# Attention and a mixture of experts on one core: the transposes of the attention take a float32r identity, and VectorE rounds a pair's k

## The chip, the cores and the metric

The kernel runs on one core of one Trainium2 chip. A core has five engines that run side by side, each with an instruction queue of its own: TensorE (PE; its weight loads are listed apart as PEld), VectorE (DVE), ScalarE (ACT), GpSimd (POOL) and SyncE (SP, which here only issues DMAs). The metric is the device time of one launch in microseconds (us).

## The reference

Eight batches of eight heads (sequence 576, head size 64) go through a causal attention with a decay: the score of query i and key j gets the sum of log f from j+1 to i added. The rows of the result then go through a mixture of eight experts, where each row takes one expert.

```
scores = matmul(q, k.T) / sqrt(D)
cum = cumsum(log(clip(f, 1e-4, 1)))
scores = where(causal, -1e9, scores + cum[..., :, None] - cum[..., None, :])
attn = exp(scores - max);  attn = attn / (sum(attn) + 1e-9)
x = matmul(attn, v)                      # 4608 rows of 512
expert = argmax(x @ w_gate);  gate = softmax(x @ w_gate)[expert]
out = gate * (relu(x @ w1[expert]) @ w2[expert])
```

All data are float32. A float32r value is a float32 word that TensorE is to take in its faster form for such words; before it is used so, an engine writes ("rounds") it in that type.

## The kernel before

**Pairs and steps.** The attention works on 32 pairs of heads, n = 0 to 31, four to a batch (p = n % 4). A pair has seven steps. In steps 0 to 4 TensorE makes the score tiles of both heads j by tile t of 128 queries: (0,3), (1,3), then (0,2) with (0,0), (1,2) with (1,0), and (0,1) with (1,1). Steps 5 and 6 make the two halves of a joint tile, which holds the last 64 queries of both heads. Each tile is the sum of two products (qk with qk, 128 rows, and k with q, 68 rows, L334), since q and k are each split in a rounded float32r part and the rest.

**What happens to a score.** VectorE's `s_red` (L341) reads the tile from PSUM, adds the mask, keeps the row's extreme and writes the tile to the buffer `sc` in SBUF. ScalarE's `s_exp` (L348) takes the exponential in place. One pair later TensorE transposes the tile in blocks of 128 x 128 (L402, L421, L432, L443: six groups of four and one single block per pair), and VectorE or ScalarE copies the transposed blocks from PSUM to `aT` (L391, L393). Another pair later `av` multiplies them with v (L472), and ScalarE copies the result to `xT` (L481). When a batch is done, its `xT` is transposed (L510, five groups of four per batch), scaled by VectorE (L520) and written out; its gate logits, `gT`, are transposed too (L560, five blocks per batch), and small operations of VectorE route the rows (L817 to L915).

**Operands.** For a later pair GpSimd rounds q (L289), takes the rest of q (L250), and copies the rounded q (L298). ScalarE rounds k (`k_first`, L293), and only then can GpSimd take the rest of k (L250, in `copies`). GpSimd's queue has these four in that order for each pair, and five more operations per batch for the routing (L897).

**Order.** The order of all work on each engine is the order in which the code issues it (`order.pin`). In a step, the code issues the scores of pair n, then the transposes of pair n-1, then the exponentials; k_first of pair n+1 comes at the end of step 1, ahead of `av`.

**Memory.** The score tiles of PSUM rotate through three banks (`ps_s`), the transposes through two (`ps_t`). `s_joint` puts the single transposed block of the pair before (L443) into the bank of its first half. So the second score tile of the next pair (step 1, 128x512) takes the bank that the first joint half (step 5, 128x288) leaves, once VectorE has read it.

**Experts.** From about 333 us on, TensorE runs the experts' matmuls (L1106, L1129) and transposes the gathered rows in groups of four; there the identity is float32r already (`identr`, L1071).

Of the kernel before, what the change touches and what calls it, by code (L numbers as in the profile page):

```python
# [57 lines left out]
def open_pools(c, ctx, tc):  # L58


    pool = lambda name, bufs, **k: ctx.enter_context(tc.tile_pool(name=name, bufs=bufs, **k))
    c.const = pool("const", 1)
    c.rp = pool("route_c", 1)
    c.rps = pool("route_s", 1)
    c.sm = pool("att_sm", 2)
    c.qp = pool("qk", 3)
    c.wp = pool("raw", 2)
    c.sp = pool("att_s", 2)
    c.xp = pool("xT", 2)
# [20 lines left out]
def setup_consts(c, tc):  # L90
    c.ident = c.const.tile([P, P], F32, name="ident")
    make_identity(tc.nc, c.ident)


def attention_all(c, tc, qkT, va, vb, f, wgd, x_dram, batch_done, more_consts, extra):
# [19 lines left out]
    with ExitStack() as st:  # L115
# [65 lines left out]

        cw = c.xp.tile([NH, 2, 640], F32R, name="cw", tag="xT")
        cwf = cw.bitcast(F32)
# [37 lines left out]
        wg = c.const.tile([P, NPAIR, 32], F32, name="wg")  # L221
        gT = c.const.tile([P, 5 * P], F32, name="gT")

        def late_consts():
            nc.gpsimd.memset(wg, 0.0)
            nc.gpsimd.memset(gT[:, S:], 0.0)
            more_consts()
# [7 lines left out]

        vts, xTs, ssums, jsums = {}, {}, {}, {}
        vbs = [io.tile([KB, 2, HD], F32, name=f"vb_{i}", bufs=1) for i in range(3)]
# [54 lines left out]
        def k_first(n):  # L292
            nc.scalar.copy(ops[n][0][:, QW:], raws[n][:, QW:])  # L293

# [26 lines left out]

        scs, nms, aTs = {}, {}, {}

        def s_begin(n):
            scs[n] = sp.tile([P, 2 * HW + S], F32, name="sc", tag="sc")
            nms[n] = sm.tile([P, 12], F32, name="nmx", bufs=3)
# [25 lines left out]
        def s_tiles(n, items):

            b, p = divmod(n, NPAIR)
            pb = psum(ps_s)
            o = 0
            for j, t in items:
                w = P * (t + 1)
                smm(pb[:, o : o + w], n, [(j, j * 640 + P * t)], 0, w)
                o += w  # L360
            o = 0
            for j, t in items:
                w = P * (t + 1)
                d = j * HW + SO[t]
                s_red(n, d, pb[:, o : o + w], mask[:, 512 - w :], 5 * j + t, 1.0e38)
                o += w

        def e_tiles(n, items):
            b, p = divmod(n, NPAIR)
            for j, t in items:  # L370
                s_exp(n, j * HW + SO[t], P * (t + 1), 5 * j + t,
                      ssums[b][:, t, 2 * p + j : 2 * p + j + 1])

        def s_joint(n, half):
            pb = psum(ps_s)
            smm(pb[:, 0:JW], n, [(0, 512), (1, 1152)], half * JW, JW)
            if half == 0 and n > 0:

                t_last(n - 1, pb[:, JW : JW + P])
            m = mask[:, 0:JW] if half == 0 else maskj  # L380
            s_red(n, half * JW, pb[:, 0:JW], m, 10 + half,
                  1.0e38 if half == 0 else nms[n][:, 10:11])
# [30 lines left out]

        def t_one(n, eng):
            aT, sc = aTs[n], scs[n]
            pt = psum(ps_t)
            for j in range(2):
                for k in range(2):
                    s0 = j * HW + SO[1] + P * k
                    o = P * (2 * j + k)  # L420
                    note(nc.tensor.transpose(pt[:, o : o + P], sc[:, s0 : s0 + P], c.ident))  # L421
            copy_on(
                eng, aT[:, :, P : P + 2 * AS].rearrange("p j (a q) -> p j a q", q=AS)[..., 0:P],
                pt.rearrange("p (j a q) -> p j a q", j=2, a=2),
            )

        def t_joint(n, eng):
            aT, sc = aTs[n], scs[n]
            pt = psum(ps_t)
            for k in range(4):  # L430
                s0 = P * k
                note(nc.tensor.transpose(pt[:, P * k : P * k + P], sc[:, s0 : s0 + P], c.ident))  # L432
# [26 lines left out]
        def av(n):  # L459
# [3 lines left out]
            for (qa, qb, nb), bank in zip(AV, (ps_v, ps_m)):  # L463
# [40 lines left out]
        def fin_x(b, t, scalar=False):  # L504
            xT, rinv = xTs[b], rinvs[b]
# [32 lines left out]
        def fin_gate(b):  # L538

            xT = xTs[b]  # L540
            for q0, q1 in ((0, 512), (512, S)):
                g = psum(ps_s)
                for p in range(NPAIR):
# [4 lines left out]
                    ))  # L548
                nc.scalar.copy(gT[:, q0:q1], g[:, 0 : q1 - q0])

        def fin_logits(b, part, bank=None):
# [7 lines left out]
            for i, t in enumerate(tiles):  # L559
                note(nc.tensor.transpose(  # L560
                    pg[:, P * i : P * i + P], gT[:, P * t : P * t + P], c.ident
                ))
            for i, t in enumerate(tiles):
# [40 lines left out]
        def s_steps(n):  # L604
# [3 lines left out]
                      [(0, 1), (1, 1)])  # L608
            r = [(lambda g=g: (s_begin(n) if n not in scs else None, s_tiles(n, g)),
                  lambda g=g: e_tiles(n, g)) for g in groups]  # L610
            return r + [
                (lambda: s_joint(n, 0), lambda: None),
                (lambda: s_joint(n, 1),
                 lambda: s_exp(n, 0, S, 11, jsums[b][:, p : p + 1])),
            ]
# [33 lines left out]
        for n in range(NP + 2):  # L649
            b, p = divmod(n, NPAIR)  # L650
            if n < NP and p == 0:
                xTs[b] = c.xp.tile([P, NPAIR, S], F32, name="xT", tag="xT")
                ssums[b] = sm.tile([P, 5, H], F32, name="ssum")
# [93 lines left out]
def setup_routing(c, tc, B):  # L747
# [3 lines left out]
    nt = B * 5  # L751
    c.identr = c.const.tile([P, P], F32R, name="identr")
    V.tensor_copy(c.identr, c.ident)
    c.iota128 = rp.tile([P, P], F32, name="iota128")
# [215 lines left out]
class Moe:  # L970
# [65 lines left out]
    def begin_x(self, e, chunk):  # L1036
# [3 lines left out]
        else:  # L1040
            x = c.xp.tile([P, 2, KT, CB], F32R, name="xb", tag="xT")
        self.x[e, chunk] = x
# [43 lines left out]
    def begin_h(self, e, chunk):  # L1086
        c = self.c
        n = (CA, CB)[chunk]
        self.h[e, chunk] = (
            c.sp.tile([P, FT, n], F32R, name="hh", tag="sc"),  # L1090
            c.sp.tile([P, FT, n], F32R, name="hl", tag="aT"),
# [344 lines left out]
```

## Time and profile before

| What | us |
|---|---|
| three runs | 833.38, 833.59, 834.72 |
| their median | 833.59 |
| the profiled execution | 835.61 |
| its span, first to last instruction | 833.9 |
| TensorE / weight loads busy | 807.9 / 713.7 |
| VectorE / ScalarE / GpSimd busy | 464.1 / 432.7 / 390.4 |

The profiled execution is 2.0 us above the median. The mean granted clock of TensorE is 0.996 of full speed. The attention ends at about 333 us; VectorE, ScalarE and GpSimd have most of their work before that.

### The profile page before, as it was taken

How to read it: one execution, taken by the hardware profiler on the slowest of the kernel's cores; microseconds unless marked ns; L12 is line 12 of the kernel's file. 1: busy time of each engine (PE TensorE's matmuls, PEld its weight loads, DVE VectorE, ACT ScalarE, POOL GpSimd, SP SyncE). 2: the span in 40 equal slices, each digit the busy share in tenths (PEclk: the TensorE clock that was granted, in tenths of full speed). 3: DMA queues.
4: the chain of work that ended last, by engine and by line, in shares of the span. 5: the costliest groups of instructions: out<-in, count | busy, mean ns of one | idle time of the engine just before them, and what ended most of it. 6: DMA issues, size and time to landing. Idle time of an engine off the chain costs nothing. (4 is left out here: it accounts for less than half of the span.)

```text
span 833.9 us, 15405 instructions
## 1 busy us (share of the span) xinstructions
PE 807.9 (97%) x5664; PEld 713.7 (86%) x5664; DVE 464.1 (56%) x1435; ACT 432.7 (52%) x1110; POOL 390.4 (47%) x310
## 2 busy tenths in 40 slices
PE   4799999999999999999999999999999999999996
PEld 3688888888888888888989899898898998998984
DVE  6655868686868687745562545336325434544410
ACT  6889989898989899934312222122122122231210
POOL 7968797979797979652420321302203203101001
PEclk9999999999999999999999999999999999999999
DMA  7987787777777873524470541523515405304000
GB/s 169 232 193 165 177 183 176 183 170 186 166 185 168 189 168 113 177 95 156 136 237 3 177 150 39 189 101 120 151 51 164 160 1 177 122 27 151 35 26 30
DMA packets 40385, 114.65 MB, mean 137 GB/s; under 512 B 6951, under 2 KB 8999, under 8 KB 36980
## 3 DMA queue, kind: packets, MB, share of 16 engines
q1 hardware_dynamic: 33268, 93.70, 43.2%
q0 software_dynamic: 6400, 19.93, 6.6%
q8 instruction: 46, 0.75, 0.4%
q14 instruction: 31, 0.25, 0.1%
q10 hardware_dynamic: 640, 0.01, 0.0%
HBM read 94.05 MB, written 20.55 MB: 137 GB/s over the span
## 5 line engine op out<-in xcount | busy, mean ns | idle before, releaser
L1129 PE MATMUL ps<-w,hh 128*128 128x512 f32 x640 | 199.0, 395 | 0.0
L1137 POOL DMA_INDIRECT out<-y,si_fast x37 | 43.8, 1184 | 310.4 <-ACT y L1136 283.5
L348 ACT ACTIVATE sc<-sc,nmx 128x512 f32<-128x512 f32 (+4 forms) x288 | 167.3, 582 | 16.0 <-DVE nmx L341 15.8
L341 DVE CUSTOM_DVE_ANT_0 sc<-ps,mask 128x512 f32<-128x512 f32 (+4 forms) x288 | 129.9, 480 | 74.4 <-PE ps L334 74.0
L1111 ACT ACTIVATE hh<-ps 128x384 fp32r<-128x384 f32 (+1 forms) x128 | 56.1, 438 | 196.5 <-PE ps L1106 196.5
L1106 PE MATMUL ps<-xa,w 128*128 128x384 f32 x768 | 145.0, 337 | 0.1
L1112 DVE SCALAR_TENSOR_TENSOR hl<-ps,hh 128x384 fp32r<-128x384 f32 (+1 forms) x128 | 62.6, 489 | 145.7 <-ACT hh L1111 145.4
L1129 PEld LDWEIGHTS ps<-w,hh 128*128 128x128 f32 x640 | 118.1, 188 | 23.0
L334 PE MATMUL ps<-qk 128*128 128x288 f32 (+4 forms) x384 | 127.5, 363 | 10.4 <-ACT qk L275 10.3
L1106 PEld LDWEIGHTS ps<-xa,w 128*128 128x128 f32 x768 | 132.6, 188 | 1.3 <-DVE hl L1112 0.2
L1129 PE MATMUL ps<-w,hl 128*128 128x512 f32 x320 | 124.3, 393 | 0.0
L334 PE MATMUL ps<-k,q 68*128 68x288 f32 (+4 forms) x384 | 105.4, 322 | 6.1 <-DMA k<-ck 2.4
L1106 PE MATMUL ps<-xb,w 128*128 128x256 f32 x768 | 101.8, 283 | 0.3 <-DVE hl L1112 0.3
L1106 PEld LDWEIGHTS ps<-xb,w 128*128 128x128 f32 x768 | 98.9, 190 | 3.2 <-DVE hl L1112 0.4
L250 POOL TENSOR_TENSOR k<-raw,qk 64x1152 fp32r<-64x1152 f32 x30 | 79.6, 2654 | 44.0 <-ACT qk L293 38.3
L1136 ACT ACTIVATE y<-ps,g_fast 128x512 f32<-128x512 f32 x37 | 25.5, 689 | 136.0 <-PE ps L1129 130.2
L472 PE MATMUL ps<-aT,va_t 128*64 128x256 f32 (+3 forms) x896 | 94.7, 355 | 0.0
L393 ACT COPY aT<-ps 128x512 f32<-128x512 f32 (+1 forms) x156 | 83.3, 534 | 14.9 <-PE ps L402 9.9
L250 POOL TENSOR_TENSOR qk<-raw,qk 64x1280 fp32r<-64x1280 f32 x30 | 87.9, 2929 | 2.4
L982 DVE CAST w<-wraw 128x1024 fp32r<-128x1024 f32 x56 | 38.9, 702 | 82.8 <-PE ps L1129 51.8
L472 PEld LDWEIGHTS ps<-aT,va_t 128*64 128x64 f32 x896 | 59.1, 138 | 29.1 <-issue 6.0
L334 PEld LDWEIGHTS ps<-qk 128*128 128x128 f32 x384 | 69.8, 195 | 14.1 <-ACT qk L275 10.3
(162 smaller groups left out, 1134.7 us busy)
## 6 DMA issues: line engine op xcount, KB each, us to landing
wraw<-in_w SPq DMA_DIRECT2D x63, 512.0 KB
raw<-in_qkT SPq DMA_DIRECT2D x52, 608.0 KB
va_t<-in_va SPq DMA_DIRECT2D x32, 256.0 KB
x_dram<-row SPq DMA_DIRECT2D x32, 256.0 KB
raw<-in_qkT SPq DMA_DIRECT2D x12, 320.0 KB
raw<-in_qkT SPq DMA_DIRECT2D x12, 288.0 KB
vb<-in_vb SPq DMA_DIRECT2D x32, 32.0 KB
x_dram<-row SPq DMA_DIRECT2D x8, 128.0 KB
```

Source lines behind the costliest of these rows:

```text
L250: return eng.tensor_tensor(o, raws[n][p0 : p0 + 64, c0:c1], ops[n][0][p0 : p0 + 64, c0:c1].bitcast(F32), ALU.subtract,)
L334: note(nc.tensor.matmul(out, ql[:, q0 : q0 + P], kl[:, j, k0 : k0 + kw], start=(i == 0), stop=(i == last),))
L341: V.tensor_tensor_reduce(scs[n][:, dst : dst + src.shape[1]], src, m, -0.125, init, ALU.add, ALU.min, nms[n][:, col : col + 1],)
L348: nc.scalar.activation(x, x, AF.Exp, bias=nms[n][:, col : col + 1], scale=-1.0, accum_out=acc)
L393: nc.scalar.copy(dst, src)
L472: c.last_av = note(nc.tensor.matmul(pv[j * HD : (j + 1) * HD, q0 - qa : qb - qa], l, r, start=(blk == 0), stop=(blk == nb - 1),))
L982: V.tensor_copy(w[:, 0], raw)
L1106: c.note(nc.tensor.matmul(ph[:, 0:n], w[:, wi, fs], x[:, xi, kt, :], start=(k == 0), stop=(k == 3 * KT - 1),))
L1111: nc.scalar.activation(hh[:, ft, :], ph[:, 0:n], AF.Relu)
L1112: nc.vector.scalar_tensor_tensor(hl[:, ft, :], ph[:, 0:n], 0.0, hh[:, ft, :].bitcast(F32), ALU.max, ALU.subtract,)
L1129: c.note(nc.tensor.matmul(py, hi_[:, ft, ms], w[:, wi], start=(ft + k == 0), stop=(ft == FT - 1 and k == 2),))
L1137: nc.gpsimd.indirect_dma_start(out=self.out, out_offset=bass.IndirectOffsetOnAxis(ap=si[:, s : s + 1], axis=0), in_=y, in_offset=None, bou ...
```

## The change

- The score tiles, `xT` and `gT` move from rotating pools to fixed places in SBUF, each with two names over the same bytes: float32 (`values`), by which VectorE and ScalarE write and read, and float32r (`words`), by which TensorE transposes. A score buffer has seven such names by region.
- All transposes of the attention (768 + 32 of scores, 160 of `xT`, 40 of `gT`) go through `turn`: words in, the float32r identity `identr`, and the output taken as float32r.
- `identr` is written during the first setup, not in that of the routing.
- `k_first` of pairs 2 to 31 runs on VectorE.
- The experts' `xb` and `hh` use the fixed places of `xT` and `sc`.

```
+def two_named(c, nc):
+    at = -(-nc.sbuf_base // 32) * 32
+    sizes = [("sc", SCW), ("sc", SCW), ("xT", XTW), ("xT", XTW), ("gT", 5 * P)]
+    nc.alloc_sbuf_tensor("two_named", [P, sum(n for _, n in sizes)], F32)
+    c.values, c.words = {}, {}
+    def name(key, nm, n, off, values=True):
+        for kept, dt, w in ((c.values, F32, ""), (c.words, F32R, "w")):
+            if values or dt == F32R:
+                kept[key] = nc.alloc_sbuf_tensor_at(
+                    f"{nm}{w}", [P, n], dt, offset=off).ap()
...
 def setup_consts(c, tc):
     c.ident = c.const.tile([P, P], F32, name="ident")
     make_identity(tc.nc, c.ident)
+    c.identr = c.const.tile([P, P], F32R, name="identr")
+    tc.nc.gpsimd.tensor_copy(c.identr, c.ident)
...
         def k_first(n):
-            nc.scalar.copy(ops[n][0][:, QW:], raws[n][:, QW:])
+            V.tensor_copy(ops[n][0][:, QW:], raws[n][:, QW:])
...
+        def turn(out, words):
+            note(nc.tensor.transpose(out.bitcast(F32R), words, c.identr))
+
         def t_tiles(n, items, engs):
-            aT, sc = aTs[n], scs[n]
+            aT = aTs[n]
             pt = psum(ps_t)
             o = 0
             for j, t in items:
                 for k in range(t + 1):
-                    s0 = j * HW + SO[t] + P * k
-                    note(nc.tensor.transpose(pt[:, o : o + P], sc[:, s0 : s0 + P], c.ident))
+                    turn(pt[:, o : o + P], region(c.words, n, j, t)[:, P * k : P * k + P])
...
-            note(nc.tensor.transpose(pt[0:KB], scs[n][:, 512 : 512 + KB], c.ident))
+            turn(pt[0:KB], region(c.words, n, 0, -1)[:, 512 : 512 + KB])
...
             for p in range(NPAIR):
-                note(nc.tensor.transpose(
-                    px[:qn, P * p : P * p + P], xT[:, p, qs : qs + qn], c.ident
-                ))
+                turn(px[:qn, P * p : P * p + P], xT[:, p, qs : qs + qn])
```

The order of TensorE and of SyncE stays as it was. The operation that moves between engines is the rounding of k. On VectorE, at the turn from step 1 to step 2 of pair 12 (`sc`, `nmx` are the score tile and its row extremes, `pr`, `ex`, `vals` belong to the routing), the order before is:

```order
L341 ISA sc,nmx<-ps,mask 128x512
L341 ISA nmx 128x1
L341 ISA sc,nmx<-ps,mask 128x512
L341 ISA nmx 128x1
L842 TENSOR_REDUCE pr<-ex 128x5
L843 TENSOR_SCALAR pr<-pr 128x5
L844 RECIPROCAL pr<-pr 128x5
L846 CAST vals<-pr 128x5
```

The same place on VectorE after the change, where line 384 is `s_red`, line 337 `k_first` and lines 882 to 886 are the same routing operations:

```order
L384 ISA sc_03_58,nmx<-ps,mask 128x512
L384 ISA nmx 128x1
L384 ISA sc_13_64,nmx<-ps,mask 128x512
L384 ISA nmx 128x1
L337 CAST qk_1909<-raw 128x1152
L882 TENSOR_REDUCE pr<-ex 128x5
L883 TENSOR_SCALAR pr<-pr 128x5
L884 RECIPROCAL pr<-pr 128x5
```

The rounding of k (128x1152) now stands behind the second `s_red` of the pair, ahead of the routing's operations and of the `s_red` of step 2. On ScalarE, at the same place of the same pair, the order before is:

```order
L393 COPY aT<-ps 128x4x128
L348 ACTIVATE sc,ssum<-sc,nmx 128x512
L393 COPY aT<-ps 128x4x128
L348 ACTIVATE sc,ssum<-sc,nmx 128x512
L293 CAST qk_1732<-raw 128x1152
L481 COPY xT<-ps 128x256
L481 COPY xT<-ps 128x320
L824 ACTIVATE ex<-shs 128x40
```

And after the change, with line 436 for the copy to `aT`, 391 for the exponential and 524 for the copy to `xT`:

```order
L436 COPY aT<-ps 128x4x128
L391 ACTIVATE sc_03_73,ssum<-sc_03_73,nmx 128x512
L436 COPY aT<-ps 128x4x128
L391 ACTIVATE sc_13_79,ssum<-sc_13_79,nmx 128x512
L524 COPY xT_87<-ps 128x256
L524 COPY xT_87<-ps 128x320
L864 ACTIVATE ex<-shs 128x40
```

The row of the rounding is gone from ScalarE, and the copies to `xT` follow the exponential at once.

## Rows read from the trace of the kernel before

**Rows 1.** Busy time by stretch: stretch, length, PE, PEld, DVE, ACT, POOL (instructions), PE clock, DMA share, GB/s.
```profile
46.00:330.00 284.00, 284.00 (x2531) 243.92 (x2528) 211.80 (x917) 260.37 (x720) 236.57 (x159) 1.00 0.74 174
```

**Rows 2.** Timeline of TensorE, pair 15 to 16: start, duration, instruction, count, [idle before].
```profile
176.68 0.43 PE L334 MATMUL ps<-k,q 68*128 68x288 f32 x2
176.94 0.60 PE L432 MATMUL ps<-ident,sc 128*128 128x128 f32 x4
177.30 0.48 PE L334 MATMUL ps<-qk 128*128 128x512 f32 x1
...
178.28 0.47 PE L334 MATMUL ps<-qk 128*128 128x512 f32 x1
```

**Rows 3.** Timeline of TensorE among the experts' matmuls, columns as before.
```profile
575.01 0.40 PE L1129 MATMUL ps<-w,hl 128*128 128x512 f32 x1
575.25 0.46 PE L1071 MATMUL ps<-identr,xg 128*128 128x128 f32 x4
575.54 0.70 PE L1129 MATMUL ps<-w,hh 128*128 128x512 f32 x2
```

**Rows 4.** Timeline of VectorE, the first joint half of pairs 12 to 15.
```profile
145.39 0.45 DVE L341 CUSTOM_DVE_ANT_0 sc<-ps,mask 128x288 f32<-128x288 f32 x1
...
155.96 0.39 DVE L341 CUSTOM_DVE_ANT_0 sc<-ps,mask 128x288 f32<-128x288 f32 x1
...
167.50 0.45 DVE L341 CUSTOM_DVE_ANT_0 sc<-ps,mask 128x288 f32<-128x288 f32 x1
...
177.48 0.45 DVE L341 CUSTOM_DVE_ANT_0 sc<-ps,mask 128x288 f32<-128x288 f32 x1
```

**Rows 5.** Timeline of TensorE, the second score tile of pairs 13 to 15.
```profile
146.33 0.48 PE L334 MATMUL ps<-qk 128*128 128x512 f32 x1
...
157.14 0.48 PE L334 MATMUL ps<-qk 128*128 128x512 f32 x1
...
168.62 0.48 PE L334 MATMUL ps<-qk 128*128 128x512 f32 x1
```

**Rows 6.** Timeline of VectorE, one copy to aT of pair 15's step 2.
```profile
174.38 0.29 DVE L391 COPY aT<-ps 128x128 f32<-128x128 f32 x1 [0.19 <-ACT aT L393]
```

**Rows 7.** Groups by line and form: count, busy us, mean ns, idle before by releaser.
```profile
L982 DVE CAST w<-wraw 128x1024 fp32r<-128x1024 f32 x56 | 38.9, 702 | 82.8 <-PE ps L1129 51.8 <-DMA wraw<-in_w 26.2 <-PE ps L1106 2.6
```

**Rows 8.** Timeline of VectorE: s_red of step 2, pair 13; of steps 1, 2, pair 15.
```profile
151.11 0.56 DVE L341 CUSTOM_DVE_ANT_0 sc<-ps,mask 128x384 f32<-128x384 f32 x1 [2.32 <-PE ps L334]
...
169.81 0.68 DVE L341 CUSTOM_DVE_ANT_0 sc<-ps,mask 128x512 f32<-128x512 f32 x1
...
173.41 0.56 DVE L341 CUSTOM_DVE_ANT_0 sc<-ps,mask 128x384 f32<-128x384 f32 x1 [1.20 <-PE ps L334]
```

**Rows 9.** Timeline of VectorE, pair 16: end of step 1, the routing, s_red of step 2.
```profile
179.38 0.69 DVE L341 CUSTOM_DVE_ANT_0 sc<-ps,mask 128x512 f32<-128x512 f32 x1
...
183.05 0.56 DVE L341 CUSTOM_DVE_ANT_0 sc<-ps,mask 128x384 f32<-128x384 f32 x1 [0.26 <-PE ps L334]
```

**Rows 10.** Timeline of GpSimd, pairs 15 and 16.
```profile
173.03 2.65 POOL L250 TENSOR_TENSOR k<-raw,qk 64x1152 fp32r<-64x1152 f32 x1 [3.16 <-ACT qk L293]
175.64 1.24 POOL L289 CAST qk<-raw 128x1280 fp32r<-128x1280 f32 x1
176.96 2.93 POOL L250 TENSOR_TENSOR qk<-raw,qk 64x1280 fp32r<-64x1280 f32 x1
179.95 1.24 POOL L298 CAST q<-raw 64x1280 fp32r<-64x1280 f32 x1
```

**Rows 11.** Timelines of GpSimd and VectorE in the setup.
```profile
14.84 0.29 POOL L773 CAST onesb<-of 128x128 bf16<-128x128 f32 x1
15.44 1.43 POOL L778 CAST trib<-trif 128x128 bf16<-128x128 f32 x1
...
15.19 1.53 DVE L250 TENSOR_TENSOR qk<-raw,qk 64x1280 fp32r<-64x1280 f32 x1
```

**Rows 12.** Timeline of TensorE, the last wait of the start.
```profile
41.95 0.48 PE L334 MATMUL ps<-k,q 68*128 68x512 f32 x1 [2.42 <-DMA k<-ck]
```

More of the change, by code (lines that the diff above doesn't have):

```diff
@@ L79, in open_pools, with region @@
     c.ps_m = pool("ps_m", 1, space=PSUM)
+JOINT = S + 8
+SO = {3: JOINT, 2: JOINT + 512, 0: JOINT + 896, 1: JOINT + 1024}
+HW = 1280
+SCW = JOINT + 2 * HW
+XTW = NPAIR * S
+REGIONS = [("J", 0, JOINT)] + [
+    (f"{j}{t}", j * HW + SO[t], n) for j in range(2) for t, n in ((3, 512), (2, 512), (1, 256))
+]
+def two_named(c, nc):
[8 more added lines that the diff above has]
+                    f"{nm}{w}", [P, n], dt, offset=off).ap()
+    for i, (nm, n) in enumerate(sizes):
+        if nm == "sc":
+            name(("sc", i), f"sc{i}", n, at, False)
+            for r, o, rn in REGIONS:
+                name((i, r), f"sc{i}_{r}", rn, at + 4 * o)
+        elif nm == "xT":
+            name(("xT", i - 2), f"xT{i - 2}", n, at)
+        else:
+            for k, (a, z) in enumerate(((0, 512), (512, 640))):
+                name(("gT", k), f"gT{k}", z - a, at + 4 * a)
+        at += 4 * n
+def region(names, n, j, t):
+    r, o = ("J", 0) if t < 0 else (f"{j}{2 if t == 0 else t}", 384 if t == 0 else 0)
+    return names[n % 2, r][:, o:]
 def psum(pool):
@@ L180, in attention_all @@
             scan(cum[hs, cs], fr[hs, 512:S], cum[hs, 511:512])
-        cw = c.xp.tile([NH, 2, 640], F32R, name="cw", tag="xT")
+        cw = c.words["xT", 0][0:NH, 0:1280].rearrange("p (r s) -> p r s", r=2)
         cwf = cw.bitcast(F32)
@@ L221, in attention_all @@
         wg = c.const.tile([P, NPAIR, 32], F32, name="wg")
-        gT = c.const.tile([P, 5 * P], F32, name="gT")
+        gTs, gTw = ([t["gT", k] for k in range(2)] for t in (c.values, c.words))
         def late_consts():
             nc.gpsimd.memset(wg, 0.0)
-            nc.gpsimd.memset(gT[:, S:], 0.0)
+            nc.gpsimd.memset(gTs[1][:, S - 512 :], 0.0)
+            for i in range(2):
+                nc.gpsimd.memset(c.values[i, "J"][:, S:], 0.0)
             more_consts()
@@ L320, in c_rows @@
                 sp_dma(q2c[:, 640:], r)
-        scs, nms, aTs = {}, {}, {}
+        nms, aTs = {}, {}
         def s_begin(n):
-            scs[n] = sp.tile([P, 2 * HW + S], F32, name="sc", tag="sc")
             nms[n] = sm.tile([P, 12], F32, name="nmx", bufs=3)
@@ L380, in s_joint @@
             m = mask[:, 0:JW] if half == 0 else maskj
-            s_red(n, half * JW, pb[:, 0:JW], m, 10 + half,
+            s_red(n, region(c.values, n, 0, -1)[:, half * JW :], pb[:, 0:JW], m, 10 + half,
                   1.0e38 if half == 0 else nms[n][:, 10:11])
@@ L540, in fin_gate @@
             xT = xTs[b]
-            for q0, q1 in ((0, 512), (512, S)):
+            for gT, (q0, q1) in zip(gTs, ((0, 512), (512, S))):
                 g = psum(ps_s)
@@ L548, in fin_gate @@
                     ))
-                nc.scalar.copy(gT[:, q0:q1], g[:, 0 : q1 - q0])
+                nc.scalar.copy(gT[:, 0 : q1 - q0], g[:, 0 : q1 - q0])
         def fin_logits(b, part, bank=None):
@@ L559, in fin_logits @@
             for i, t in enumerate(tiles):
-                note(nc.tensor.transpose(
-                    pg[:, P * i : P * i + P], gT[:, P * t : P * t + P], c.ident
-                ))
+                turn(pg[:, P * i : P * i + P], gTw[part][:, P * i : P * i + P])
             for i, t in enumerate(tiles):
@@ L608, in s_steps @@
                       [(0, 1), (1, 1)])
-            r = [(lambda g=g: (s_begin(n) if n not in scs else None, s_tiles(n, g)),
+            r = [(lambda g=g: (s_begin(n) if n not in nms else None, s_tiles(n, g)),
                   lambda g=g: e_tiles(n, g)) for g in groups]
@@ L651, in attention_all @@
             if n < NP and p == 0:
-                xTs[b] = c.xp.tile([P, NPAIR, S], F32, name="xT", tag="xT")
+                xTs[b], xTws[b] = (
+                    t["xT", (b + 1) % 2].rearrange("p (n s) -> p n s", s=S)
+                    for t in (c.values, c.words)
+                )
                 ssums[b] = sm.tile([P, 5, H], F32, name="ssum")
@@ L751, in setup_routing @@
     nt = B * 5
-    c.identr = c.const.tile([P, P], F32R, name="identr")
-    V.tensor_copy(c.identr, c.ident)
     c.iota128 = rp.tile([P, P], F32, name="iota128")
@@ L1040, in begin_x @@
         else:
-            x = c.xp.tile([P, 2, KT, CB], F32R, name="xb", tag="xT")
+            x = c.words["xT", (e + 1) % 2][:, 0 : 2 * KT * CB].rearrange(
+                "p (i k s) -> p i k s", i=2, k=KT)
         self.x[e, chunk] = x
@@ L1089, in begin_h @@
         self.h[e, chunk] = (
-            c.sp.tile([P, FT, n], F32R, name="hh", tag="sc"),
+            c.words["sc", chunk][:, 0 : FT * n].rearrange("p (f n) -> p f n", n=n),
             c.sp.tile([P, FT, n], F32R, name="hl", tag="aT"),
@@ L1340, in tile_attention_moe @@
     c.nc = nc
+    two_named(c, nc)
     open_pools(c, ctx, tc)
```

30 lines of the change are left out of this document (12 added, 18 removed).

## The prediction

> **What bounds the kernel now.** I read the busy shares by stretch first. Between 46 and 330 us, the steady part of the attention, TensorE is listed busy for 284.00 of 284.00 us, ScalarE for 260.37, GpSimd for 236.57 and VectorE for 211.80 [rows 1]. So nothing comes sooner there unless TensorE's queue gets shorter. But its ends are modelled, so a full row can hide waits. I therefore set TensorE's timeline beside VectorE's and asked at each score group when its bank of PSUM came free. One place is tight: the second score tile of a pair takes the bank that the first joint half of the pair before leaves. In pair 15 VectorE ends that half at 177.48 + 0.45 = 177.93 [rows 4], and TensorE starts the tile at 178.28 [rows 2], 0.35 later. No start in the stretch is nearer, so 0.35 is the handover, and what a start lies beyond it is reserve. By pair of the batch, from rows 4 and 5:
> - p = 3 (pair 15): no reserve; the tile waits for VectorE already.
> - p = 0 (pair 12): 145.39 + 0.45 = 145.84, start 146.33, so 0.49, reserve 0.14 [rows 4, 5].
> - p = 1 (pair 13): 156.35 to 157.14, 0.79, reserve 0.43 [rows 4, 5].
> - p = 2 (pair 14): 167.95 to 168.62, 0.67, reserve 0.32 [rows 4, 5].
>
> VectorE's own chain up to that point starts with the `s_red` of step 2, which waits for TensorE (2.32 us in pair 13, 1.20 in pair 15 [rows 8], 0.26 in pair 16 [rows 9]). From there it runs on without a gap but one: 0.19 us ahead of a small copy to `aT`, behind ScalarE's copy of the same transposes [rows 6]. So the attention has two bounds with little between them: TensorE's queue, and VectorE's chain from step 2 to step 5 of each pair.
>
> **The change: the transposes.** In the float32 form a group of four ends 0.43 us after the matmul before it: 176.68 + 0.43 = 177.11, 176.94 + 0.60 = 177.54. The matmul behind it then takes its usual 0.24 (177.30 + 0.48 = 177.78) [rows 2]. With the float32r identity the group ends 0.30 after (575.41 to 575.71), but the two matmuls behind it end at 576.24, 0.53 for what takes 0.48; the next weight load comes late by the difference. So the group costs about 0.36 [rows 3]. To the third digit of the starts and ends this is 0.442 against 0.365: **0.077 saved per group of four**, 0.136 where two groups stand together, 0.10 for one of five, nothing for the single block (I charge 0.01). I take this as the same for scores, `xT` and `gT`, since all are 128 x 128 blocks. The bounds: nothing at all (the float32 pace stays), and 0.13, if what follows did not pay (0.43 - 0.30).
>
> Per pair TensorE's queue gets shorter by six groups of four, 6 x 0.077 - 0.01 = 0.45. In p = 0 and 1 two groups of `xT` join in: 2 x 0.136 + 4 x 0.077 - 0.01 = 0.57. In p = 2 it is one group of `xT`, four blocks of `gT` and a fifth: 2 x 0.136 + 3 x 0.077 + 0.10 - 0.01 = 0.59.
>
> **Where VectorE takes it back.** VectorE's chain has a start that moves with TensorE, but gains from the faster transposes only at its one gap: the last group ahead of it ends some 0.11 sooner, so the chain is shorter by 0.11, and the 0.08 of the last group lies behind the gate. Where the gate has no reserve, a pair gains 0.11 + 0.08 = 0.19 and not 0.45. So p = 3 gains **0.19**, and so do pairs 3, 4 and 5, whose gate has no reserve either. In p = 2, TensorE is sooner by 0.52 ahead of the gate, the chain by 0.11, the reserve is 0.32; a wait of 0.09 appears, and the pair gains **0.51**. In p = 1 the reserve covers it: **0.57**.
>
> **The rounding of k on VectorE.** VectorE rounds 128 x 1024 in 0.70 us [rows 7], so 1152 in some 0.76, 0.70 of it added to the queue behind what overlaps. It stands right behind the second `s_red`, so it has the idle time ahead of the `s_red` of step 2 to hide in. That is 2.32 us in p = 1 and 1.20 in p = 3 [rows 8], and in p = 2 VectorE has nothing else between the two: hidden. In p = 0 the routing's operations fill the place and 0.26 is left [rows 9]. The `s_red` of step 2 comes late there by some 0.53, and so does the chain: 0.53, less the 0.19 of its gap, is 0.34 later. TensorE meanwhile is 0.50 sooner ahead of the gate. With the reserve of 0.14 a wait of 0.34 + 0.50 - 0.14 = 0.70 appears, against 0.57 or 0.58 gained: p = 0 **loses 0.12**. Were the rounding free, it would gain 0.25.
>
> ScalarE loses 30 roundings; no wait of TensorE in the stretch ends with it alone, so I give nothing for that. GpSimd's k rest starts sooner, as it waits for the rounding now (3.16 us in pair 15 [rows 10]); nobody waits for GpSimd in the stretch, so nothing again. The early `identr` and the two small fills of GpSimd lie ahead of the last wait of the start, 2.42 us for a DMA at 41.95 [rows 12]; it also swallows what pairs 0 to 2 would gain or lose. The experts' use of the fixed places makes ScalarE wait for reads of the expert before, long done.
>
> **The sum.** Pairs 3 to 30 hold p = 2 seven times, the others six times, and pairs 3 to 5 apart: 7 x 0.51 + 6 x 0.57 + 6 x 0.19 - 6 x 0.12 + 3 x 0.19 = 8.0. Behind pair 30, twelve groups of scores, five of `xT` and the last `gT` stand between matmuls with no gate: 17 x 0.077 + 0.2 = 1.5. That is 9.5 us: the profiled execution goes from 835.61 to 826.1. That execution is 2.0 above the median of 833.59, so the median goes to **824.1**; I say 824.5, since a lost tenth per gated pair is likelier than a won one.
>
> **Rivals.**
> *The full gain.* If VectorE's chain does not gate (say it catches up with ScalarE's load gone), every group counts: per four pairs 0.57 + 0.57 + 0.59 + 0.45 = 2.18, over pairs 3 to 30 some 15.0, with the end 16.5: 817.1. Against it is the handover of 0.35 with no reserve in p = 3 [rows 2, 4], which the change leaves in place.
> *Slower: GpSimd holds VectorE up.* VectorE and GpSimd got in each other's way in the setup: a GpSimd cast of a form that takes 0.29 us took 1.43 while VectorE's subtraction of 1.53 ran [rows 11]. If a running GpSimd operation holds the rounding just so, p = 0 pays one to one, six times over; the gain of 9.5 is gone at 1.58 us per pair. GpSimd's copy of q (1.24) gives back 7.4 (831.5); its rest of q, 2.93 [rows 10], would cost 17.6: 841.7. In the old order the copy of q stands at 179.95 to 181.19 [rows 10], just where the rounding of pair 16 would start (180.07 [rows 9]). But the rounding in p = 3 would now end at 169.81 + 0.68 [rows 8] + 0.76 = 171.25, and GpSimd's rest of k start then, not at 173.03 behind a wait of 3.16 for ScalarE [rows 10]. Its four operations (2.65 + 1.24 + 2.93 + 1.24 = 8.06, some 0.2 between them) end at 179.5, 0.5 ahead of the next rounding. So that finds GpSimd idle, waiting for it. [...]
> *No faster transposes.* If the weight load alone set the pace, at the float32 pace, TensorE would save nothing, and only p = 0 would pay for the rounding: 0.34 - 0.14 = 0.20 six times, 834.8. [...]
>
> **Chances.** The forecast has 0.62, the full gain 0.14. GpSimd's hold has 0.12: 0.05 for the copy of q, 0.07 for more. No faster transposes has 0.06; 0.06 is left for what I have not seen, half of it no change, half slower. A measurement of this kernel can tell about 0.2%, 1.7 us: faster is below 831.9, slower above 835.3. So faster has 0.62 + 0.14 + half of the 0.05, and a little for partial holds: 0.79; the same 0.11; slower 0.10. The likeliest case alone spans 821 (0.10 more per gated pair and the rounding of p = 0 hidden) to 828 (groups at 0.05 instead of 0.077). The range reaches from the full gain to the hold by the copy of q: 816.5 to 832.
>
> **What would show it.** Right: a group of four transposes of scores ends about 0.30 after the matmul before it; VectorE's rounding takes 0.76; the second score tile starts 0.35 behind the joint half in p = 3, 0 and 2, but later than that in p = 1; the `s_red` of step 2 in p = 0 follows the routing without idle time. Wrong: a rounding far above 0.76, or starting late behind a GpSimd operation; groups of transposes that still take 0.43; a second score tile that starts less than 0.35 behind the joint half; or a gain in the experts' part, where I expect none.

## The result, and the profile after

The changed kernel takes 823.55 us (four runs, 823.14 to 824.35), the kernel before 834.15 beside it: a ratio of 0.9871, 95% interval 0.9853 to 0.9890, or 10.6 us less (9 to 12 by the interval). The profiled execution took 823.85 us with a span of 822.1, 11.8 less than the profiled execution before.

The first line of the page (engine, busy us, share, instructions), and two stretches of the kernel after, columns as in [rows 1]:

```profile
PE 797.0 (97%) x5664; PEld 700.3 (85%) x5664; DVE 494.1 (60%) x1465; ACT 401.4 (49%) x1080; POOL 390.6 (48%) x312
```
```profile
46.00:330.00 284.00, 282.07 (x2628) 239.08 (x2625) 245.77 (x987) 244.41 (x729) 250.39 (x166) 1.00 0.77 183
42.00:47.00 5.00, 4.97 (x46) 3.68 (x46) 3.02 (x11) 4.70 (x13) 4.11 (x3) 1.00 0.96 195
```

In the same 284 us TensorE gets through 2628 instructions, not 2531. VectorE is now at 245.77 and ScalarE at 244.41: the two have changed places.

**Where the time came from.** TensorE's 5664 instructions have one order in both kernels, so the start of each can be set against the start of the same one before. First the kernel before, at four points of TensorE's timeline (start, duration): the last matmuls of pair 1's product with v, the second score tile of pair 31, the first waited-for transpose among the experts, the last group:

```profile
46.97 0.22 PE L472 MATMUL ps<-aT,vb 68*64 68x64 f32 x2
...
337.60 0.48 PE L334 MATMUL ps<-qk 128*128 128x512 f32 x1
...
396.09 0.26 PE L1071 MATMUL ps<-identr,xg 128*128 128x128 f32 x1 [0.44 <-DMA xg<-x_dram,gi_fast]
...
820.27 0.39 PE L1129 MATMUL ps<-w,hh 128*128 128x512 f32 x1
```

The same four instructions after:

```profile
45.40 0.23 PE L516 MATMUL ps<-aT,vb 68*64 68x64 f32 x2
...
324.52 0.47 PE L377 MATMUL ps<-qk 128*128 128x512 f32 x1
...
381.90 0.25 PE L1112 MATMUL ps<-identr,xg 128*128 128x128 f32 x1 [0.41 <-DMA xg<-x_dram,gi_fast]
...
808.48 0.39 PE L1170 MATMUL ps<-w,sc1w 128*128 128x512 f32 x1
```

The lead, by which the same instruction starts sooner, is 1.57 us at the end of the start, 13.08 at pair 31, 14.19 at the experts and 11.79 at the end. So in these two executions the start gave 1.6, the pairs 11.5, the end of the attention 1.1, and **the experts took 2.4 back**. How much of the start's part is the change's stays open, as the runs below show.

**The gate.** VectorE's first joint half of pairs 12 to 15 after the change, then the second score tile of pairs 13 to 16 on TensorE (they answer to [rows 2, 4, 5]):

```profile
140.59 0.45 DVE L384 CUSTOM_DVE_ANT_0 sc_J<-ps,mask 128x288 f32<-128x288 f32 x1
...
150.74 0.39 DVE L384 CUSTOM_DVE_ANT_0 sc_J<-ps,mask 128x288 f32<-128x288 f32 x1
...
161.59 0.45 DVE L384 CUSTOM_DVE_ANT_0 sc_J<-ps,mask 128x288 f32<-128x288 f32 x1
...
170.98 0.45 DVE L384 CUSTOM_DVE_ANT_0 sc_J<-ps,mask 128x288 f32<-128x288 f32 x1
```
```profile
141.39 0.47 PE L377 MATMUL ps<-qk 128*128 128x512 f32 x1
...
151.49 0.47 PE L377 MATMUL ps<-qk 128*128 128x512 f32 x1
...
162.40 0.47 PE L377 MATMUL ps<-qk 128*128 128x512 f32 x1
...
171.78 0.47 PE L377 MATMUL ps<-qk 128*128 128x512 f32 x1
```

The starts lie 0.35, 0.36, 0.36 and 0.35 behind the ends: all four kinds of pairs stand at the handover, with no reserve left. Pairs p = 0 to 3, from one second score tile to the next, took 10.26, 10.81, 11.48 and 9.66 us, and take 10.14, 10.10, 10.91 and 9.38: gains of 0.12, 0.70, 0.57 and 0.28, together 1.67. By the savings per group that the starts show (below), TensorE's queue is shorter by 0.66, 0.82, 0.65 and 0.48, together 2.6: the rest stands at the gate. (The expectation of the lighter VectorE below counts 2.49, with 0.66 for p = 1; the double group of p = 1 in which the transposes of the last 64 rows of `xT` load 64 columns saves 0.27 us.)

**The rounding of k.** VectorE's roundings in pair 12 (p = 0) and pair 14 (p = 2), with the last routing operation and the `s_red` of step 2 of pair 12 between them and that of pair 14 behind, and then GpSimd's work beside the two roundings:

```profile
132.96 0.76 DVE L337 CAST qk<-raw 128x1152 fp32r<-128x1152 f32 x1
...
136.25 0.17 DVE L926 SCALAR_TENSOR_TENSOR pr<-pr,hi 128x5 f32<-128x5 f32 x1
136.33 0.55 DVE L384 CUSTOM_DVE_ANT_0 sc<-ps,mask 128x384 f32<-128x384 f32 x1
...
153.24 2.14 DVE L337 CAST qk<-raw 128x1152 fp32r<-128x1152 f32 x1
...
157.24 0.56 DVE L384 CUSTOM_DVE_ANT_0 sc<-ps,mask 128x384 f32<-128x384 f32 x1 [1.86 <-PE ps L377]
```
```profile
131.76 1.25 POOL L342 CAST q<-raw 64x1280 fp32r<-64x1280 f32 x1
...
151.84 2.93 POOL L294 TENSOR_TENSOR qk<-raw,qk 64x1280 fp32r<-64x1280 f32 x1
```

The first takes the 0.76 us of the estimate; GpSimd's copy of q ends at 133.01, 0.05 after it began. The second takes 2.14. GpSimd's rest of q runs to 154.77 there, and the rounding ends 0.61 after that, nearly as if it had begun only then. VectorE is still idle for 1.86 us behind it, until TensorE's next scores, so nothing waits.

### The profile page after: what moved, and what is told of

It reads as the page before. It is cut to its first block, busy times and chain, and to the rows that moved or that the text cites. A ratio compares the mean times of both kernels' runs of the same rounds, so it can differ in the third digit from the quotient of the medians.

```text
span 822.1 us, 15505 instructions
## 1 busy us (share of the span) xinstructions
PE 797.0 (97%) x5664; PEld 700.3 (85%) x5664; DVE 494.1 (60%) x1465; ACT 401.4 (49%) x1080; POOL 390.6 (48%) x312
## 5 line engine op out<-in xcount | busy, mean ns | idle before, releaser
L391 ACT ACTIVATE sc<-sc,nmx 128x512 f32<-128x512 f32 (+3 forms) x256 | 142.5, 558 | 12.2 <-DVE nmx L384 11.0
L377 PE MATMUL ps<-qk 128*128 128x288 f32 (+4 forms) x384 | 126.4, 360 | 12.8 <-ACT qk L319 10.6
L384 DVE CUSTOM_DVE_ANT_0 sc<-ps,mask 128x512 f32<-128x512 f32 (+3 forms) x256 | 115.1, 484 | 34.7 <-PE ps L377 34.0
L1170 PE MATMUL ps<-w,sc0w 128*128 128x512 f32 x384 | 119.8, 397 | 0.0
L1153 DVE SCALAR_TENSOR_TENSOR hl<-ps,sc0w 128x384 fp32r<-128x384 f32 x64 | 35.6, 556 | 85.5 <-ACT sc0w L1152 85.5
L377 PEld LDWEIGHTS ps<-qk 128*128 128x128 f32 x384 | 70.4, 197 | 19.1 <-ACT qk L319 10.6
L1152 ACT ACTIVATE sc0w<-ps 128x384 fp32r<-128x384 f32 x64 | 31.4, 491 | 106.0 <-PE ps L1147 106.0
L1170 PEld LDWEIGHTS ps<-w,sc0w 128*128 128x128 f32 x384 | 70.2, 188 | 12.9
L1170 PE MATMUL ps<-w,sc1w 128*128 128x512 f32 x256 | 80.2, 395 | 0.0
L377 PEld LDWEIGHTS ps<-k,q 68*128 68x128 f32 x384 | 72.6, 199 | 2.0 <-POOL q L314 1.6
```

The source lines that it names most:

```text
L377: note(nc.tensor.matmul(out, ql[:, q0 : q0 + P], kl[:, j, k0 : k0 + kw], start=(i == 0), stop=(i == last),))
L384: V.tensor_tensor_reduce(dst[:, 0 : src.shape[1]], src, m, -0.125, init, ALU.add, ALU.min, nms[n][:, col : col + 1],)
L391: nc.scalar.activation(x, x, AF.Exp, bias=nms[n][:, col : col + 1], scale=-1.0, accum_out=acc)
L1152: nc.scalar.activation(hh[:, ft, :], ph[:, 0:n], AF.Relu)
L1153: nc.vector.scalar_tensor_tensor(hl[:, ft, :], ph[:, 0:n], 0.0, hh[:, ft, :].bitcast(F32), ALU.max, ALU.subtract,)
L1170: c.note(nc.tensor.matmul(py, hi_[:, ft, ms], w[:, wi], start=(ft + k == 0), stop=(ft == FT - 1 and k == 2),))
```

## The experiments

Each was timed beside the kernel before. Ratios are to it. Where the intervals of two runs overlap (those of after, of the other places and of the lighter VectorE do), their difference rests on the traces, set side by side.

**The transposes alone** (`words_k_act`), the kernel after with

```
         def k_first(n):
-            V.tensor_copy(ops[n][0][:, QW:], raws[n][:, QW:])
+            nc.scalar.copy(ops[n][0][:, QW:], raws[n][:, QW:])
```

> Only the transposes change: as after, but ScalarE rounds k again at its old place. Theory A (VectorE's chain from step 2 to step 5 gates every pair; the rounding costs only in p = 0, where it makes the s_red of step 2 0.45 us late): p = 0 pairs go from 10.14 us to some 9.86, so 7 x 0.28 = 2.0 us less than after in the steady part; the start goes back to the waits of before (some 1.6 us more); in all 823 us, within 0.2% of after. Theory B (ScalarE's relief of 30 x 1.05 us is what pays): several us slower than after, 828 or more, with waits for ScalarE's copies.

Measured: 827.48 us, 0.9927 (0.9909 to 0.9946), some 4 us slower than after. Neither theory had that number. A was wrong on p = 0, which takes 10.09 us (9.86 expected); the waits for ScalarE's copies that B named are there. The loss is in p = 3 (9.74 against 9.38) and p = 1 (10.28 against 10.10). At step 2 of pair 15 VectorE's, ScalarE's and TensorE's timelines show:

```profile
168.64 0.29 DVE L434 COPY aT<-ps 128x128 f32<-128x128 f32 x1 [0.42 <-ACT aT L436]
...
166.36 1.14 ACT L337 CAST qk<-raw 128x1152 fp32r<-128x1152 f32 x1
167.40 0.70 ACT L524 COPY xT<-ps 128x256 f32<-128x256 f32 x2
...
168.12 0.49 ACT L436 COPY aT<-ps 128x384 f32<-128x384 f32 x1
...
167.24 0.50 PE L440 MATMUL ps<-identr,sc_02w 128*128 128x128 f32 x4
```

The transposes end at 167.74, but ScalarE, behind its rounding and two copies, starts its copy at 168.12, and VectorE's small copy waits 0.42 us for that one, 0.07 in after: 0.35 more, where the pair takes 0.36 more. In p = 1 the wait is 0.24 for 0.07, and the pair takes 0.18 more. VectorE's chain, which gates, runs through ScalarE.

**The rounding alone** (`k_dve_only`), the kernel before with the line above the other way round.

> Only the rounding moves: as before, float32 transposes, but VectorE rounds k. Theory A: the gate of p = 0 has 0.14 us reserve and the chain gets at most that much longer, p = 1 to 3 hide the rounding; the steady part is unchanged within 1 us, and 833 to 835 us in all. Theory B: a large part of the 10.6 us is here, 828 or less. In the experts' part the matmuls of 512 columns stand 232 ns apart if the placement of the fixed memory made them 234 in the profile after, and 234 if that came from the chip or the execution.

Measured: 832.85 us, 0.9994 (0.9984 to 1.0004), no change, as A said. In the pairs its lead over before stays at 1.4 to 1.5 us from pair 12 to 31: VectorE hides the rounding, and nothing there gets shorter. The two edits apart give some 6 us and nothing; together 10.6.

**The fixed places with float32 transposes** (`placed_f32_turn`):

```
         def turn(out, words):
-            note(nc.tensor.transpose(out.bitcast(F32R), words, c.identr))
+            note(nc.tensor.transpose(out, words.bitcast(F32), c.ident))
```

> As after (fixed places, k rounded by VectorE), but the transposes of the attention take the float32 identity and the float32 name. Theory A: like the rounding alone, plus what the fixed places cost in the experts' part: 234 ns between matmuls of 512 columns and some 2.4 us more than the rounding alone, 835 to 837 us. If the places cost nothing: the same time as the rounding alone within 0.5 us.

Measured: 835.00 us, 1.0015 (1.0006 to 1.0025): 2.1 us over the rounding alone. After differs from this run in the form of the transposes alone and is 11.5 us faster: the gain comes with them. The same two instructions of the experts, on TensorE's timeline, first in the rounding alone, then here:

```profile
394.64 0.25 PE L1071 MATMUL ps<-identr,xg 128*128 128x128 f32 x1 [0.45 <-DMA xg<-x_dram,gi_fast]
...
818.61 0.39 PE L1129 MATMUL ps<-w,hh 128*128 128x512 f32 x1
```
```profile
393.61 0.26 PE L1112 MATMUL ps<-identr,xg 128*128 128x128 f32 x1 [0.34 <-DMA xg<-x_dram,gi_fast]
...
819.97 0.39 PE L1170 MATMUL ps<-w,sc1w 128*128 128x512 f32 x1
```

423.97 us against 426.36 (before 424.18, after 426.58). So the experts' 2.4 us come with the fixed places, not with the transposes. In this run, as in after, the 808 neighbouring starts of 512-column matmuls lie 234.0 to 234.1 ns apart, against 232.2; 747 of 256 columns 120.5 against 119.8.

**Other places** (`placed_32`):

```
-SCW = JOINT + 2 * HW
+SCW = -(-(JOINT + 2 * HW) // 32) * 32
...
-    at = -(-nc.sbuf_base // 32) * 32
+    at = -(-(nc.sbuf_base - 32) // 128) * 128 + 32
...
-    nc.alloc_sbuf_tensor("two_named", [P, sum(n for _, n in sizes)], F32)
+    nc.alloc_sbuf_tensor("two_named", [P, sum(n for _, n in sizes) + 16], F32)
```

> As after, but the fixed places start 32 bytes later and the score buffers are padded, so that sc0, sc1 and both xT start at 32 modulo 128 bytes, as the pool's buffers did before (in after sc0 starts at 0 and xT at 64 modulo 128); the rest keeps its place modulo 128. If the start's alignment makes the matmuls that load from sc0 slow (237.4 ns apart, 234.8 from sc1, 233.8 from the pool before): sc0 and sc1 both go to 234 to 235, some 1 to 2.4 us off the experts' part, 821.5 to 822.5. If the region of SBUF is the cause: 237 and 235 again, 823.5.

Measured: 821.76 us, 0.9855 (0.9833 to 0.9877), some 2 us faster than after. The experts' two instructions stand at:

```profile
382.19 0.25 PE L1112 MATMUL ps<-identr,xg 128*128 128x128 f32 x1 [0.38 <-issue]
...
806.21 0.39 PE L1170 MATMUL ps<-w,sc1w 128*128 128x512 f32 x1
```

424.02 us, as before the change, but not by the way that was expected. The 512-column matmuls still lie 233.9 ns apart and keep 1.25 us of their loss; those of 256 columns, whose moving operand lies in the place of `xT`, went to 118.2 ns and take 1.2 us less than before. Neighbours that both load from `sc0` went from 237.2 to 236.9 ns, those from `sc1` from 234.7 to 232.0; the same instructions lay 235.7 and 230.5 apart before, so the 233.8 of the expectation mixes a slower and a faster buffer, and `sc0` was slow already. That the place counts is shown. The alignment modulo 128 bytes as the rule is not: by the places that the expectation gives and the sizes in the code `sc0` went from 0 to 32 and kept its pace, while `sc1` stood at 32 in both runs and got faster.

**A lighter VectorE** (`t_one_act`), the kernel after with the copy of step 4 on ScalarE:

```
-                lambda: t_one(n, "v"),
+                lambda: t_one(n, "s" if n else "v"),
```

> As after, but the copy of the transposed (0,1) and (1,1) tiles (128x512, step 4) goes from VectorE to ScalarE for pairs 1 to 31: 0.61 us less in VectorE's chain ahead of the gate. Theory A: the gate opens in all four kinds of pairs, TensorE's queue is left as the bound, and the waits that remained (2.49 us of shorter queue per four pairs, 1.69 of it won) go: 0.8 x 6.75 = 5 us faster than after, 818.5. Theory C (TensorE's queue is the bound already, the handover of 0.35 is a coincidence): no change, 823.5. Should ScalarE become the bound instead: slower than after, with TensorE waiting for ScalarE's copies.

Measured: 821.43 us, 0.9848 (0.9829 to 0.9868). The gate opens in all four kinds of pairs (reserves 0.26, 0.46, 0.50 and 0.32 us in pairs 12 to 15), which no theory of a coincidence allows. Four pairs take 39.97 us, not 40.53. But only 2 of the 5 us come: p = 0 stays at 10.11, and the lead at the end of the start is -0.1, 1.7 less than in after. The expectation of a later run puts that down to a wait of 3.6 us for VectorE's copy; most of it comes after that wait, with a lower clock (the stretch in this run, columns as in [rows 1]):

```profile
32.00:38.00 6.00, 6.00 (x34) 4.08 (x34) 3.11 (x5) 3.46 (x9) 5.24 (x3) 0.50 1.04 260
```

The granted clock is 0.50 to the end of that stretch; after has 1.00 on record from 35.3 us on. VectorE's rounding and GpSimd's copy of q in pair 12:

```profile
133.46 1.38 DVE L337 CAST qk<-raw 128x1152 fp32r<-128x1152 f32 x1
...
132.98 1.24 POOL L342 CAST q<-raw 64x1280 fp32r<-64x1280 f32 x1
```

The faster pairs bring the copy of q, to 134.22, into the rounding, which now takes 1.38 us.

**The rounding among GpSimd's work** (`k_at_step0`), the kernel after with

```
-                if i == 1 and 0 < n and n + 1 < NP:
+                if i == 0 and 0 < n and n + 1 < NP:
                     k_first(n + 1)
```

> As after, but VectorE rounds k one step earlier, behind the s_red of step 0, where GpSimd is still at its work on q (in the trace of after its copy of q ends 0.04 us behind the start of the rounding in p = 0). If a running GpSimd operation holds VectorE's rounding (as the 2.13 us in p = 2 of after, against 0.76 in the other pairs, looks): roundings of 1.3 to 2.5 us in p = 0 and 3, the s_red of step 2 later by the hold, 6 to 14 us more than after: 830 to 838. If not (the 2.13 has another cause, such as VectorE's own queue): 0.76 each, and 823 to 824.

Measured: 829.74 us, 0.9943 (0.9920 to 0.9965), 6 us slower than after; in the trace 5.0 of that lie in the pairs. VectorE's rounding and GpSimd in pair 11 (p = 3):

```profile
125.57 1.68 DVE L337 CAST qk<-raw 128x1152 fp32r<-128x1152 f32 x1
...
125.38 1.24 POOL L342 CAST q<-raw 64x1280 fp32r<-64x1280 f32 x1
```

It ends 0.63 us after GpSimd's copy (126.62), like the one of p = 2 in after, and those of p = 2 take 2.75. Pairs p = 3 take 9.99 us and p = 2 11.26. p = 0 was not hit (0.76). So a rounding that starts 1.05 us before the end of GpSimd's copy is held to 1.68 us; the one of p = 0 in after, which starts 0.05 before that end, takes 0.76.

**ScalarE rounding later** (`k_act_step2`), the transposes alone with k_first at the end of step 2; the rest of k and the load of a later pair go to step 3.

```
-                    elif i == 2:
+                    elif i == 3:
                         copies(n + 1)
...
-                if i == 2 and 0 < n < NP - 3:
+                if i == 3 and 0 < n < NP - 3:
                     load_pair(n + 3)
...
-                if i == 1 and 0 < n and n + 1 < NP:
+                if i == 2 and 0 < n and n + 1 < NP:
                     k_first(n + 1)
```

> As the transposes alone (ScalarE rounds k, 827.5), but ScalarE does it at the end of step 2, behind its copy of the transposed tile of step 2, not ahead of it; GpSimd's rest of k and the load of a later pair follow a step later. If the transposes alone lost 4 us against after because ScalarE's copy came late and VectorE's small copy waited for it (0.24 to 0.42 us of wait in p = 0, 1, 3, against 0.07): that wait goes back to 0.07 at step 2 and appears at most at step 3; 824 to 825.5. If ScalarE's load as such is the cause: no better than 827. If GpSimd's rest of k comes too late for the next pair: TensorE waits for k, 830 or more.

Measured: 879.50 us, 1.0538 (1.0512 to 1.0563): the third case. TensorE's waits (waiting line, releaser, us in total, times, longest):

```profile
PE ps L377 <- POOL k L294: 19.8, 30, 2.6
```

The small copy's wait at step 2 did go to 0.07 us (and one of 0.7 to 0.8 appeared at step 3), but the rest of k came too late in every pair, so this run says nothing on how much ScalarE's lateness costs. Its mean granted clock is 0.969, that of the transposes alone 0.995, so the 52 us between them need not all be those waits.

**GpSimd's copy of q behind its rest of k** (`q_copy_behind`), the kernel after with

```
-            nc.gpsimd.tensor_copy(q2[0:64], raws[n][0:64, 0:QW])
             lo(nc.gpsimd, n, k2[0:64].rearrange("p j s -> p (j s)"), 0, QW, QW + 2 * S)
+            nc.gpsimd.tensor_copy(q2[0:64], raws[n][0:64, 0:QW])
```

> As after, but GpSimd takes the rest of k first and copies the rounded q behind it, so that it stands idle, waiting for the rounding, when VectorE comes to round k. In after the rounding of p = 0 and 3 is 0.76 us already and only that of p = 2 is held (2.13 us, by the rest of q, with 4 us of idle time to hide in), so the time should stay within 0.2% of after: 822.5 to 824.5. If the copy of q behind the rest of k made the next pair's operands late: slower, with TensorE waiting for q.

Measured: 823.87 us, 0.9870 (0.9847 to 0.9892): the time of after, as expected.

**The gains together.** `placed_32_t_one_act` has the other places and the copy of step 4 on ScalarE from pair 4 on; `placed_32_t_one_act_q` has GpSimd's order of the last run too.

> The places of the run before, and the copy of step 4 on ScalarE from pair 4 on (that copy on ScalarE from pair 1 on gave 821.4, but lost 1.7 us at the start to a wait of 3.6 us for VectorE's copy). If both gains add and the start is left alone: 821.4 - 1.7 - 1.5 = 818. If the places cost nothing: 819.7. If the start's loss comes in any case: 821.

Measured: 819.75 us, 0.9823 (0.9803 to 0.9843). The lead at the end of the start is only 0.2 us all the same, so 818 was too good. But `placed_32` has 1.3 there, and up to there the two runs do the same work in the same order. What differs is the pace of TensorE, here at pair 0's product with v, first in `placed_32`, then in this run:

```profile
34.15 2.50 PE L516 MATMUL ps<-aT,va_t 128*64 128x256 f32 x16
```
```profile
34.23 3.47 PE L516 MATMUL ps<-aT,va_t 128*64 128x256 f32 x16
```

The same 16 matmuls take 1.0 us more: the granted clock is 1.00 from 35.5 us on there and from 37.9 here. So a lead at the start belongs to the execution as much as to the kernel, and moving the copy did not cost it.

> The run with both the places and the copy of step 4 on ScalarE, and GpSimd's copy of q behind its rest of k. In that run the faster pairs brought GpSimd's copy of q into the rounding of p = 0 and 3: it took 1.3 to 1.5 us instead of 0.76, and p = 0 had 10.1 us where its shorter queue would allow 9.6. If the hold is that loss: roundings of 0.76 in p = 0 and 3, pairs p = 0 0.4 to 0.5 us shorter, 3 us in all: 816.5. If p = 0 is bound by the routing on VectorE anyway: 819.7 as before.

Measured: 817.80 us, 0.9795 (0.9775 to 0.9815), the fastest of all, 16 us under the kernel before. VectorE's rounding in pair 12:

```profile
131.50 0.81 DVE L337 CAST qk<-raw 128x1152 fp32r<-128x1152 f32 x1
```

It is 0.81 again, and p = 0 takes 9.84 us, not 10.07 (pair 16: 9.82, not 10.29). So the hold was part of the loss of p = 0. Of the 2.6 us between the two spans (818.6 and 816.0) the pairs gave some 1.3, less than the 3 expected; 1.4 came at the start, whose lead is 1.6 us again, and are not shown to be this edit's.

What holds p = 0 at 9.84, where its shorter queue would allow 9.6, stands in the same trace: on ScalarE the moved copy and the copy of the joint tile of step 6, on TensorE the weight load of the transposes of step 1, which take the bank of PSUM that the second copy reads:

```profile
128.71 0.58 ACT L436 COPY aT<-ps 128x512 f32<-128x512 f32 x1
...
130.17 0.58 ACT L436 COPY aT<-ps 128x512 f32<-128x512 f32 x1
...
130.81 0.39 PEld L440 LDWEIGHTS ps<-identr,sc_13w 128*128 128x128 f32 x4 [0.42 <-ACT aT L436]
```

The copy of the joint tile starts 0.72 us behind its transposes, 0.31 in after, where the other copy is not in ScalarE's queue. From the last matmul of the scores to the first of `av` it then takes 0.84 us, 0.62 in after: that is the 0.2. So the copy that opened the gate makes TensorE wait once in four pairs. Those take 39.75 us, 2.46 less than before, of some 2.6 by which the queue is shorter.

## Why the prediction was right, and where its terms were off

The forecast (824.5, and a sum of 9.5 us) stands beside 823.55 and 11.8 us in the profiled executions. Its mechanism held, but the sum came near by luck, through errors that partly cancel: start +1.6, pairs +3.5, end of the attention -0.4, experts -2.4. The medians lie 10.6 apart, not 11.8, as the profiled execution before lay 1.5 above the median beside the changed kernel, the one after 0.3; by that estimate most of the start's 1.6 is theirs and not the change's.

**The price of a group: right.** On TensorE's timeline after, around a group of the joint tile:

```profile
41.20 0.42 PE L377 MATMUL ps<-k,q 68*128 68x288 f32 x2
41.47 0.46 PE L440 MATMUL ps<-identr,sc_Jw 128*128 128x128 f32 x4
41.76 0.47 PE L377 MATMUL ps<-qk 128*128 128x512 f32 x1
42.07 0.40 PE L377 MATMUL ps<-k,q 68*128 68x512 f32 x1
```

The group ends at 41.93, 0.31 behind the matmul before it, and the next ends at 42.23, 0.30 later where 0.24 is usual: 0.37 for 0.44 before [rows 2]. From start to start over the pairs a group saved 0.055 to 0.08 us by its place (0.077 forecast), two together mostly 0.14 to 0.15 (0.136). The rival of no faster transposes is out. **Mis-sized:** the group ahead of `av` saves some 0.14, not 0.077. The matmuls behind it load 64 columns, not 128, and do not pay: in pair 16 the lead goes from 6.50 to 6.64 us over the group and is still 6.64 behind `av`. That is 28 x 0.065 = 1.8 us on TensorE's queue that the sum had at nothing. The double group of p = 1 that turns the last 64 rows of `xT` saves 0.27, not 0.136.

**The gate: right as a bound, its sizes off.** The handover of 0.35 held in every pair, and the full gain did not come. p = 3 and p = 2 gained 0.28 and 0.57 (0.19 and 0.51 forecast), mostly by the group ahead of `av`, which lies behind the gate. p = 1 gained 0.70 for 0.57 by the same group and that double group; its queue is shorter by 0.82, the reserve that was to cover it is used up, and the start lies 0.36 behind, so the forecast that p = 1 starts later than 0.35 was wrong. p = 0 gained 0.12, where a loss of 0.12 was forecast. The step that failed is "0.53, less the 0.19 of its gap, is 0.34 later". The `s_red` of step 2 follows the routing without idle time, as forecast, but is 0.45 late, and the chain took up 0.29 of that with its gap; its last link, 5.03 us behind the matmuls of step 2 before, is 5.19 behind them after, 0.16 later. Over four pairs the forecast was 1.15 and the trace has 1.67.

**The rounding: 0.76 us, and hidden in p = 1 to 3, right.** The order on GpSimd held by luck: its copy of q was done 0.05 after the rounding of p = 0 began, where 0.5 ahead was forecast, and a little faster pairs (the lighter VectorE) brought the two together. The rival of GpSimd's hold is real as a mechanism (2.14 us in p = 2 of after, 1.68 in p = 3 one step earlier) and was not met where it costs. The trace before shows the other direction alone [rows 11]; these runs show this one: the held roundings end 0.61 to 0.63 us behind GpSimd's operation (the first one and that of pair 14 in after, pair 12 of the lighter VectorE, pair 11 of the rounding among GpSimd's work).

**"I give nothing" for ScalarE's relief: wrong as a step.** Alone the relief is worth nothing (the rounding alone, 0.9994), but the transposes alone win 4 us less: the 0.11 that VectorE's chain was to gain needs ScalarE's copy at once, and with the rounding in its queue that copy comes late. This is read from the waits of the traces (0.35 longer in p = 3, the pair 0.36); the run that was to test it, ScalarE rounding later, failed for another reason.

**"It also swallows what pairs 0 to 2 would gain or lose": wrong for these two executions.** After, VectorE's first rounding takes 2.28 us and ends 0.62 behind GpSimd's rest of q (22.64 to 25.56), and TensorE waits 1.11 us for a copy that stands behind it. Then a matmul that takes 0.47 at 41.76 (above) takes 0.76:

```profile
23.90 2.28 DVE L337 CAST qk<-raw 128x1152 fp32r<-128x1152 f32 x1 [0.18 <-DMA raw<-in_qkT]
...
27.68 0.34 PE L440 MATMUL ps<-identr,sc_01w 128*128 128x128 f32 x1 [1.11 <-DVE aT L434]
...
30.93 0.76 PE L377 MATMUL ps<-qk 128*128 128x512 f32 x1
```

TensorE is some 3 us late by pair 2, by the wait and by this slower pace. That a lower clock is behind the pace is an estimate: in the kernel before a matmul of this form takes 0.77 at 42.62, where the granted clock falls to 0.50 (below). This trace has the clock on record only from 35.3 us on; a view of an earlier stretch prints 1.00 there. The wait of 2.42 us at 41.95 [rows 12] then does not come, and neither does what followed it. The stretch behind it, and a part of that stretch, in the kernel before, columns as in [rows 1]:

```profile
42.00:47.00 5.00, 5.00 (x29) 3.46 (x31) 1.40 (x4) 3.60 (x7) 1.34 (x2) 0.66 0.92 196
43.00:46.00 3.00, 3.00 (x14) 1.81 (x15) 0.86 (x4) 2.60 (x7) 0.40 (x1) 0.50 0.92 191
```

The granted clock is 0.66 there on the mean and 0.50 from 43 to 46 us, behind a wait of 2.42 us; in the kernel after it is 1.00 in the same 5 us. These 5 us hold 29 matmuls before and 46 (not all the same) after. So both executions lost time at the start to waits and a slower TensorE, the one before 1.6 us more. That this is the change's doing is not shown: the transposes alone, whose rounding is ScalarE's as before, have a lead of 2.5 at the same place, and `placed_32` and `placed_32_t_one_act`, with the same start, 1.3 and 0.2.

**"The experts' use of the fixed places": only a wait was looked for.** There is none, but the matmuls lie 0.2 to 0.8% farther apart, 2.4 us in all.

Open are why the place of an operand changes the distance between matmuls, and what the change is worth at the start.

## What to carry to other kernels

Before you price a faster operation by its count, find the place where its engine waits for another, and price the other engine's chain to that place: here 2.6 us of shorter queue per four pairs became 1.67, and a copy moved off that chain gave another 0.56. Two edits can be worth more together than apart (here 6 us and nothing, together 10.6), where the one opens the gate that the other runs into. Before you credit a change with a difference at the start, compare executions that do the same work there: here two of them differ by 1.2 us. When operands move to other places in memory, compare the distances of untouched matmuls before and after, far from the change.

## What had not been expected of the hardware

- The matmuls' distance changed with the places of their operands: 512 columns, 232.2 ns before and 234.1 after; 256 columns, 119.8, 120.6 and, with other places, 118.2.
- A rounding on VectorE that takes 0.76 us took 1.38, 1.68 and 2.14 where a GpSimd operation ran on for 0.76, 1.05 and 1.53 us from its start, and ended 0.61 to 0.63 behind that operation. With 0.05 of the operation left it took 0.76.
- Behind one wait of 2.42 us TensorE's granted clock was 0.66 over 5 us, and 0.50 in three of them.
- The same start did not run at the same clock in two executions: the granted clock was 1.00 from 35.5 us on in one and from 37.9 in the other, and the same 16 matmuls took 2.50 and 3.47 us.
